# A one-element copy on GpSimd that waits for a key transfer, taken out ahead of the weight loads

## The chip, the core and the metric

The kernel runs on one core of a Trainium2 chip. The metric is the device time of one execution in microseconds; lower is better. A core has five engines that run their own instruction queues side by side: TensorE (PE, with its weight loads listed apart as PEld), VectorE (DVE), ScalarE (ACT), GpSimd (POOL) and SyncE (SP). Transfers between device memory and the on-chip buffer are issued from a queue of an engine (here nearly all from GpSimd's) and carried by 16 DMA engines.

## What is computed

A block-sorted attention followed by a gated feed-forward block. Batch 4, 8 heads, 768 positions in 8 blocks of 96, head size 64; then 3,072 tokens, width 512, hidden width 1,536.

```python
P = sort_net                                   # 4 x 8 x 8 x 8
for _ in range(5):                             # Sinkhorn
    P = exp(P - max(P)); P = P / rowsum(P); P = P / colsum(P)
k_sorted = einsum('bhij,bhjcd->bhicd', P, k_b)  # blocks of keys are mixed
v_sorted = einsum('bhij,bhjcd->bhicd', P, v_b)  # blocks of values are mixed
attn = softmax(scale * q_b @ k_sorted^T)        # inside each block
x = (attn @ v_sorted) as [3072 tokens, 512]
out = (silu(x @ w_gate) * (x @ w_val)) @ w_out
```

## The kernel before

The feed-forward works on eight tiles of 384 tokens (`ffn(n)`, n = 0 to 7: two for each batch). For each of 12 columns m of 128 hidden units it runs a gate product (`gate`, line 387), a value product (`value`, line 405), each four matmuls, with tanh on ACT (line 395) and two products on DVE (lines 397 and 410). The output products of tile n-1 (`outp`, line 422) are strewn between the columns of tile n, and so are the attention steps of the tiles that come next.

Ahead of the first tile stands an opening of some 22 us: the Sinkhorn steps on ACT and DVE, meanwhile the values of batch 0 land and are turned into a column-major copy `vch` by ACT (lines 203 to 220) and by GpSimd (lines 150 to 152). TensorE then mixes the values (`v_chunk`, line 277) and the keys (`k0_chunk`, line 266), and goes on to scores, softmax and the first columns of the feed-forward (`early`, line 521).

The order of the instructions of TensorE and GpSimd is the order in which they are written. Up to line 539 that of DVE and ACT is too; from line 540 on `manual_schedule` names TensorE and GpSimd alone, and DVE and ACT are ordered by the planner.

GpSimd's queue is the one to follow here. In order: two loads of batch 0's values (lines 144 and 145), the identity matrix, the first part of the queries (`load_q0(0)`), two loads of the keys of batch 0 (`k0`, lines 148 and 149, 384 KB each), three value copies (lines 150 to 152), a copy of one element per partition out of `k0` into a tile `landed` (line 154) that nothing reads, and then the transfers that follow: `load_gv` brings 256 columns of the gate weights and of the value weights (256 KB each, line 111), six such pairs in all, between them the second part of the queries (line 156), the values of batch 1 (line 159), and behind them keys and queries of batch 1 and the output weights (lines 162 to 164). A column pair m, m+1 of the feed-forward needs the pair of loads m/2: m = 8 and 9 need the fifth pair, m = 10 and 11 the sixth.

A transfer is issued in the queue's order. Each uses one of eight completion semaphores in turn, so in the profile a later issue can be seen to wait for a transfer eight places ahead: the issue at 24.12 us waits for the second part of the queries, issued at 16.35.

GpSimd comes back to copying values when those of batch 1 have landed (lines 597 and 598), and then issues the loads for batches 2 and 3.

Of the kernel before, what the change touches and what calls it, by code (L numbers as in the profile page):

```python
# [10 lines left out]
BF16 = mybir.dt.bfloat16  # L11
# [6 lines left out]
def kernel(  # L18
# [11 lines left out]
    nc = tc.nc  # L30

    B, H, S, D = q.shape
# [21 lines left out]
    const = ctx.enter_context(tc.tile_pool(name="const", bufs=1))  # L54
# [58 lines left out]
    def load_gv(lo, hi):  # L113
        load_w(wg_sb, wg_dram, lo, hi)
        load_w(wv_sb, wv_dram, lo, hi)

    def copy_v(eng, pair, rows, s, n=4, d0=0, d1=D):
        cs = slice(s * (C // n), (s + 1) * (C // n))
        dst = vch3[rows, d0:d1, cs]
        src = v_tiles[pair][rows, cs, d0:d1]  # L120
        if eng is nc.scalar:
            eng.copy(dst, src.transpose([0, 2, 1]))  # L122
        else:
            eng.tensor_copy(dst, src.transpose([0, 2, 1]))  # L124
# [8 lines left out]
    HC = C // 2  # L133
# [3 lines left out]
    k0 = qk0[:, 0:HC, :]  # L137
# [12 lines left out]
    copy_v(nc.gpsimd, 0, lowr, 0)  # L150
    copy_v(nc.gpsimd, 0, lowr, 3)
    copy_v(nc.gpsimd, 0, lowr, 5, 8, 40, D)
    landed = const.tile([128, 1], BF16)
    nc.gpsimd.tensor_copy(landed, k0[:, HC - 1, D - 1:D])
    load_gv(0, 256)
    load_q0(1)
    for m in range(256, 1024, 256):
# [499 lines left out]
```

## Time and profile before

| | us |
|---|---|
| median of 3 runs | 249.78 |
| lowest and highest of them | 249.61 and 251.17 |
| profiled execution, its own time | 251.09 |
| its span, first to last instruction | 249.0 |
| TensorE busy | 237.3 |
| VectorE busy | 157.7 |
| ScalarE busy | 110.7 |
| GpSimd busy | 52.1 |

The profile shows one execution. The span is counted from the first instruction to the last; the execution's own time is 2.1 us longer. Views that are used below: the page's busy times and its row of 40 slices (each digit a busy share in tenths), the chain of waits (followed back from the last instruction to what released each step), the timeline of one engine (start, length, and in brackets the idle time ahead with what ended it), and a table of busy times by stretch. Line numbers are those of the kernel.

The granted TensorE clock is 1.00 over the whole span.

### The profile page before, as it was taken

How to read it: one execution, taken by the hardware profiler on the slowest of the kernel's cores; microseconds unless marked ns; L12 is line 12 of the kernel's file. 1: busy time of each engine (PE TensorE's matmuls, PEld its weight loads, DVE VectorE, ACT ScalarE, POOL GpSimd, SP SyncE). 2: the span in 40 equal slices, each digit the busy share in tenths (PEclk: the TensorE clock that was granted, in tenths of full speed). 3: DMA queues.
4: the chain of work that ended last, by engine and by line, in shares of the span. 5: the costliest groups of instructions: out<-in, count | busy, mean ns of one | idle time of the engine just before them, and what ended most of it. 6: DMA issues, size and time to landing. Idle time of an engine off the chain costs nothing.

```text
span 249.0 us, 6163 instructions
## 1 busy us (share of the span) xinstructions
PE 237.3 (95%) x2609; PEld 140.8 (57%) x2633; DVE 157.7 (63%) x332; ACT 110.7 (44%) x186; POOL 52.1 (21%) x46
## 2 busy tenths in 40 slices
PE   6799998999999999999999999999999999999995
PEld 5375655676555556654555655555555555555543
DVE  6786888787556765857558547745764585446700
ACT  3977752353643444545742552353344343232411
POOL 5966439990039400000000000000000000000000
PEclk9999999999999999999999999999999999999999
DMA  5959999999999389110112121112111121100122
GB/s 98 211 72 181 212 192 219 198 223 217 213 175 187 64 184 156 35 42 3 45 32 74 45 74 34 43 42 73 37 42 45 32 61 58 42 14 32 42 80 89
DMA packets 39578, 24.38 MB, mean 98 GB/s; under 512 B 27712, under 2 KB 35648, under 8 KB 39104
## 3 DMA queue, kind: packets, MB, share of 16 engines
q0 software_dynamic: 21376, 14.16, 38.9%
q1 hardware_dynamic: 18176, 9.84, 14.6%
q8 instruction: 20, 0.33, 0.5%
q14 instruction: 6, 0.05, 0.0%
HBM read 28.32 MB, written 7.86 MB: 145 GB/s over the span
## 4 chain that ended last, share of the span: by engine, by line
PE 72%; DMA 14%; DVE 6%; issue 3%; POOL 3%; ACT 2%; DVEq 0%; POOLq 0%
PE o_ps L422 22%; PE v_ps L405 21%; PE g_ps L387 20%; DMA wv_sb<-in_moe_w_val_dram 6%; DMA qk<-in_k_dram 4%; DMA wg_sb<-in_moe_w_gate_dram 4%; PE tkq L246 3%; PE av_ps L336 2%; DVE gs_sb L397 2%; PE qk L309 2%; DVE h L410 1%; PE o_ps L438 1%; DVE st L342 1%; ACT th_sb L395 1%; DVE vt L224 1%
## 5 line engine op out<-in xcount | busy, mean ns | idle before, releaser
L397 DVE SCALAR_TENSOR_TENSOR gs_sb<-th_sb,g_ps 128x384 bf16<-128x384 bf16 x96 | 52.9, 551 | 51.8 <-ACT th_sb L395 48.9
L405 PE MATMUL v_ps<-xt,wv_sb 128*128 128x384 bf16 x380 | 77.3, 326 | 1.4 <-DMA wv_sb<-in_moe_w_val_dram 0.8
L387 PE MATMUL g_ps<-xt,wg_sb 128*128 128x384 bf16 x376 | 76.7, 326 | 1.1 <-DMA wg_sb<-in_moe_w_gate_dram 1.0
L395 ACT ACTIVATE th_sb<-g_ps 128x384 bf16<-128x384 f32 x96 | 47.1, 491 | 57.8 <-PE g_ps L387 53.9
L422 PE MATMUL o_ps<-wo_sb,h 128*128 128x512 bf16 x255 | 61.4, 379 | 1.3 <-issue 0.3
L410 DVE SCALAR_TENSOR_TENSOR h<-v_ps,gs_sb 128x384 bf16<-128x384 f32 x96 | 53.4, 556 | 7.0 <-PE v_ps L405 0.3
L405 PEld LDWEIGHTS <-wv_sb 128*128 128x128 bf16 x380 | 35.1, 97 | 25.3 <-issue 2.0
L387 PEld LDWEIGHTS <-wg_sb 128*128 128x128 bf16 x376 | 34.7, 97 | 24.6 <-DMA wg_sb<-in_moe_w_gate_dram 1.4
L422 PEld LDWEIGHTS <-h 128*128 128x128 bf16 x276 | 26.3, 98 | 28.9
L427 ACT COPY o_sb<-o_ps 128x512 f32<-128x512 f32 x23 | 13.5, 586 | 50.8 <-PE o_ps L422 50.8
L124 POOL COPY vch<-v 64x1536 bf16<-64x1536 bf16 (+2 forms) x11 | 28.6, 2648 | 20.8 <-PE o_ps L422 17.2
L322 ACT ACTIVATE e_all<-qk 96x768 bf16<-96x768 f32 x30 | 22.6, 802 | 7.7 <-PE qk L309 7.7
L342 DVE TENSOR_TENSOR st<-av_ps,r_sb 96x512 bf16<-96x512 f32 x32 | 21.7, 679 | 0.2
L336 PEld LDWEIGHTS <-e_all 96*128 96x128 bf16 x256 | 12.2, 98 | 4.9 <-ACT e_all L322 0.8
L336 PE MATMUL av_ps<-vt,e_all 96*128 96x65 bf16 x256 | 13.5, 194 | 0.1
L340 DVE RECIPROCAL r_sb<-av_ps 96x8 f32<-96x8 f32 x32 | 6.4, 199 | 8.8 <-PE av_ps L336 8.7
L224 DVE CAST vt<-tv 96x1024 bf16<-96x1024 f32 (+1 forms) x9 | 9.8, 1100 | 2.6 <-PE tv L287 1.6
L226 ACT CAST vt<-tv 96x1024 bf16<-96x1024 f32 (+1 forms) x9 | 9.2, 1031 | 2.9 <-PE tv L287 1.8
L448 PE MATMUL idle_ps<-warm_sb 128*128 128x512 bf16 x22 | 6.1, 381 | 0.3 <-issue 0.2
L224 DVE COPY oh_sb<-o_ps 128x256 f32<-128x256 f32 x1 | 0.4, 425 | 9.3 <-PE o_ps L438 9.3
L372 POOL DMA_DIRECT2D q_scr<-in_q_dram x2 | 5.7, 3225 | 0.0
L122 ACT COPY vch<-v 64x768 bf16<-64x768 bf16 (+1 forms) x4 | 5.4, 1389 | 0.2 <-DMA v<-in_v_dram 0.2
(81 smaller groups left out, 135.0 us busy)
## 6 DMA issues: line engine op xcount, KB each, us to landing
out_dram<-o_sb SPq DMA_DIRECT2D x23, 256.0 KB, 2.0
v<-in_v_dram POOLq DMA_DIRECT2D x3, 768.0 KB, 19.6
wg_sb<-in_moe_w_gate_dram POOLq DMA_DIRECT2D x6, 256.0 KB, 10.5
wv_sb<-in_moe_w_val_dram POOLq DMA_DIRECT2D x6, 256.0 KB, 11.4
wo_sb<-in_moe_w_out_dram POOLq DMA_DIRECT2D x1, 1536.0 KB, 24.0
kp<-in_k_dram POOLq DMA_DIRECT2D x2, 768.0 KB, 14.8
q_scr<-in_q_dram POOLq DMA_DIRECT2D x2, 768.0 KB, 29.7
v<-in_v_dram POOLq DMA_DIRECT2D x2, 384.0 KB, 5.5
```

The costliest lines, as they stand in the source:

```text
L124: eng.tensor_copy(dst, src.transpose([0, 2, 1]))
L224: nc.vector.tensor_copy(dst, src)
L322: nc.scalar.activation(e_all[:, n:n + 2, 0:4 * C], wide[0:C, :, 0:4 * C], AF.Exp, scale=scale)
L336: nc.tensor.matmul(o[:, two, i4, :], lhsT=e[:, i4 * C:i4 * C + 128], rhs=vt[:, 2 * g + two, half * 4 + i4, :], start=True, stop=True)
L342: nc.vector.tensor_tensor(st.rearrange("p i two d -> p two i d"), o[0:C, :, :, 0:D], r_sb.to_broadcast([C, 2, 4, D]), op=ALU.mult)
L387: nc.tensor.matmul(g_ps, lhsT=wg_sb[:, kc, ts(m, 128)], rhs=xt[:, kc, :], start=(kc == 0), stop=(kc == NKC - 1))
L395: nc.scalar.activation(th_sb, g_ps, AF.Tanh, scale=0.5)
L397: nc.vector.scalar_tensor_tensor(gs_sb, th_sb, 1.0, g_ps, op0=ALU.add, op1=ALU.mult)
L405: nc.tensor.matmul(v_ps, lhsT=wv_sb[:, kc, ts(m, 128)], rhs=xt[:, kc, :], start=(kc == 0), stop=(kc == NKC - 1))
L410: nc.vector.scalar_tensor_tensor(h_tiles[n][:, m, :], v_ps, 0.5, gs_tiles.pop(m), op0=ALU.mult, op1=ALU.mult)
L422: nc.tensor.matmul(o_ps, lhsT=h_w[:, m, ts(t3, 128)], rhs=wo_sb[:, m, :], start=(m == 0), stop=(m == NFC - 1))
L427: nc.scalar.copy(o_sb, o_ps)
```

## The change

The copy and the tile that it writes are taken out. The next instruction of GpSimd's queue behind the last value copy is then the first weight load.

```diff
     copy_v(nc.gpsimd, 0, lowr, 0)
     copy_v(nc.gpsimd, 0, lowr, 3)
     copy_v(nc.gpsimd, 0, lowr, 5, 8, 40, D)
-    landed = const.tile([128, 1], BF16)
-    nc.gpsimd.tensor_copy(landed, k0[:, HC - 1, D - 1:D])
     load_gv(0, 256)
     load_q0(1)
     for m in range(256, 1024, 256):
```

## The prediction

> **What bounds the kernel now.** I read the page first, then the chain of waits over the first 60 us, then GpSimd's and TensorE's timelines, and a table of stretches for the DMA. The page:
>
> ```profile
> PE 237.3 (95%) x2609; PEld 140.8 (57%) x2633; DVE 157.7 (63%) x332; ACT 110.7 (44%) x186; POOL 52.1 (21%) x46
> ...
> DMA  5959999999999389110112121112111121100122
> ...
> PE 72%; DMA 14%; DVE 6%; issue 3%; POOL 3%; ACT 2%; DVEq 0%; POOLq 0%
> ```
>
> TensorE is busy for 95% of the span, so whatever is won must come out of its 11.7 us of idle time. The DMA engines are full in the first third and nearly idle after it, and yet they own 14% of the chain. The chain shows where:
>
> ```profile
> 4.06 10.16 DMA qk<-in_k_dram
> ...
> 14.35 0.19 POOL landed L154
> 14.54 0.28 issue
> 14.82 0.80 POOL wg_sb L111
> ...
> 18.38 9.46 DMA wg_sb<-in_moe_w_gate_dram
> 27.84 0.28 issue
> 28.12 14.88 DMA wv_sb<-in_moe_w_val_dram
> 43.00 0.04 issue
> 43.04 0.82 PE v_ps L405 x4
> ```
>
> It runs from the load of the keys through the copy to be removed, through the weight issues, and ends in a value product at 43.04 that waits for its weights. So the copy stands on the path that sets the end. GpSimd's own timeline:
>
> ```profile
> 6.25 6.24 POOL L124 COPY vch<-v 64x1536 bf16<-64x1536 bf16 x3 [1.64 <-DMA v<-in_v_dram]
> 14.35 0.19 POOL L154 COPY landed<-qk 128x1 bf16<-128x1 bf16 x1 [1.87 <-DMA qk<-in_k_dram]
> 14.82 0.80 POOL L111 DMA_DIRECT2D wg_sb<-in_moe_w_gate_dram  x1 [0.28 <-issue]
> ```
>
> The copies end at 12.49, the next transfer is issued at 14.82: 2.33 us in which nothing is issued. What the DMA engines do meanwhile (the last two columns are their mean busy share and GB/s):
>
> ```profile
> 12.50:13.00 0.50, 0.50 (x24) 0.47 (x17) 0.02 (x1) 0.35 (x1) 0.00 (x0) 1.00 0.61 123
> 14.00:14.50 0.50, 0.50 (x23) 0.50 (x20) 0.50 (x1) 0.23 (x1) 0.15 (x1) 1.00 0.00 0
> 16.00:16.50 0.50, 0.50 (x44) 0.50 (x38) 0.50 (x1) 0.28 (x2) 0.50 (x2) 1.00 0.12 14
> 17.00:17.50 0.50, 0.41 (x16) 0.41 (x17) 0.50 (x2) 0.50 (x2) 0.50 (x1) 1.00 1.43 193
> ```
>
> The keys' bulk is over at 13.0, and the engines then move next to nothing until about 16.5, some 1.6 us behind the issue at 14.82. Last, what TensorE loses to it:
>
> ```profile
> 14.95 1.97 PE L266 MATMUL tk<-rmix,qk 128*64 128x64 bf16 x96
> ...
> 37.74 0.82 PE L387 MATMUL g_ps<-xt,wg_sb 128*128 128x384 bf16 x4 [0.99 <-DMA wg_sb<-in_moe_w_gate_dram]
> ...
> 39.05 0.82 PE L405 MATMUL v_ps<-xt,wv_sb 128*128 128x384 bf16 x4
> ...
> 43.04 0.82 PE L405 MATMUL v_ps<-xt,wv_sb 128*128 128x384 bf16 x4 [0.78 <-DMA wv_sb<-in_moe_w_val_dram]
> ```
>
> These are columns 8 and 10 of the first tile. The value product of column 8 starts 0.06 us behind the transpose before it (38.66 + 0.33 = 38.99), with its weight load held by the DMA. These are TensorE's only waits for a transfer in the whole span.
>
> **What the change does to the start of the stream.** Removed: a copy of 0.19 us and its wait of 1.87, with the 0.28 behind it. What stands between a value copy and an issue isn't shown at this place. Bounds: at 47.79 an issue follows a value copy with no gap, and at 14.54 the gap is 0.28. I take 0.28, the same pair of kinds (a copy, then this very issue). So the first weight issue goes from 14.82 to 12.77 (12.49 at best): 2.05 us earlier, at most 2.33. All issues up to line 164 move with it. Those that wait for a completion eight places ahead (24.12 for the second part of the queries, 25.45, 26.78 and 28.12 for the second pair of weights and the third gate load, 33.67 for the fourth value load) wait for transfers of the same stream, which moves as well. The third value load and the fourth gate load, issued at 19.11 and 19.84, reuse the keys' two semaphores and now need a wait of their own for the keys; at 17.06 and 17.79 these have long landed (14.22), so I cost it at nothing; without that cover it would be the old 2 us on part of the stream.
>
> **Whether the stream moves as a whole.** From 17 us on the share is above 0.9 in nearly every stretch, at 180 to 220 GB/s, up to about 60 us; a full queue that starts 2.05 us earlier ends 2.05 us earlier. One thing limits this: fetches of instructions (33 GB/s in 13.5 to 14.0, 16 in 15.5 to 16.0) fall into the empty stretch now, and would share with weights then. 33 GB/s x 0.5 us and 16 x 0.5 are 25 KB, 0.12 us at 200 GB/s if spread, but up to 0.5 us if they fall on one engine, since a transfer has landed only when its last engine has. So landings move by 1.5 to 2.3 us; I take 1.9, near the row of the issue.
>
> **What TensorE wins.** Column 8's gate: weights land at about 37.7, TensorE is free at 36.75 (35.94 + 0.81); a shift of 0.99 clears it. Column 8's value: 0.06. Column 10's value: landed at 43.00, TensorE free at 42.27 (41.93 + 0.34), and by then 1.05 earlier, so at 41.22; the weights land at 41.1 with a shift of 1.9 and at 41.5 with 1.5. So 0.77 is won, or 0.5 with the smaller shift. Sum: 0.99 + 0.06 + 0.77 = 1.82 us at best, 1.5 at the low end.
>
> DVE and ACT must keep up when the gaps close. In the 10 us before (26 to 36) TensorE was busy 10.00, DVE 9.10 and ACT 5.82 with the same sort of work; in 36 to 46 they were busy 8.05, 7.38 and 2.85. DVE's 7.4 us fit into 8.2, a load of 0.9 as before; I take off 0.1 for it. That leaves 1.7.
>
> **What comes late next.** Everything TensorE meets behind this is fed by the same stream. Values of batch 1 land at 36.6 (issued 21.55, 15.0 to land), GpSimd's four copies of them run from 36.72 to 47.85, and `v_chunk` starts at 48.75: a cover of 0.90, kept when both move by 1.7 to 2. Keys and queries of batch 1 land at 46.4 and 49.7 and are used at 53.96; the output weights land at 57.7 and are used at 59.29: covers of 4 and 1.6. If one of these didn't move while TensorE did, the output weights would cost 0.1 and the values 0.8. Behind 60 us GpSimd's loads for batches 2 and 3 move with its copies, and TensorE waits for no transfer.
>
> **The keys.** They land at 14.22 and `k0_chunk` loads its first operand at 14.74, right behind the value chunks: a cover of 0.52 us. With the change the first weight bytes come about 1.6 us behind 12.77, at 14.4, past the keys' landing. I cost the keys at nothing; their bound is the rival below.
>
> **A rule against it.** The row: the issue at 15.60 runs beside a DVE cast that starts at 15.69 and takes 0.76 us, and the issue at 25.45 takes 0.74; casts out of PSUM did not slow an issue. The Trainium skill, SBUF — State Buffer, section "SBUF: two separate sides", warns that a DVE operation in a two-port mode locks GpSimd out, so that descriptors aren't written and transfers start late. The earlier issues fall beside the value casts at 12.98 to 15.50, which the old ones escaped; if the rule applied to those, the first issue would be held to 15.5 and the gain would be nothing or below. The row decides for me: no hold.
>
> **The sum.** 249.0 - 1.7 = 247.3 of span, 251.09 - 1.7 = 249.4 of this execution's own time. That execution lay 1.3 above the median; against the median of 249.78 the forecast is 248.1, 0.7% less.
>
> **The rivals.**
> (a) Half of it: the stream's last engine gains only 1 us (fetches, or DVE late in releasing PSUM). Column 10's wait stays: 0.9 won, 248.9. For it: columns 8 and 10 wait for the last of 16 engines, which no view shows. Against: share above 0.9 throughout.
> (b) Nothing, because the issues are held by DVE's casts, or the DMA engines' stretch stays empty for another reason: 249.8. Against: the 0.76 row.
> (c) The keys late. If all of the first pair of weights (512 KB, 2.6 us at 200 GB/s) went ahead of the keys' last bytes, they would land at 16.8 and TensorE would lose 2.6 - 0.5 = 2.1 in the opening, where nothing covers it, and win 1.8 later: 250.1. From a delay of 2.3 us on the change would be a loss. Against it: weights are issued 8 us after the keys, and the keys are nearly through at 13.0.
> (d) Slower: from line 540 on DVE and ACT are ordered by the planner, and an instruction fewer ahead can turn that order. One DVE product (0.56 us, lines 397 and 410) put ahead of what TensorE waits for, in each of the eight tiles, costs 4.5, less 1.7: 252.6. It is a loss from 0.21 us a tile on. For it: DVE is at 0.9 in the first tile. Against: behind 26 us the view of waits has 0.8 us of TensorE's matmuls waiting for DVE, and none for ACT.
>
> **How the numbers follow.** Forecast 0.64, (a) 0.14, (b) 0.06, (c) 0.05, (d) 0.06; 0.05 for a win above 2.5 us, by an order that fell better. A measurement of this kernel can tell about 1% (2.5 us) from no change. Within 1% lie the forecast, (a), (b) and (c): 0.89, of which I give 0.02 to slower for a mixture with (d): faster 0.05, same 0.87, slower 0.08. Range: from 1.82 + 0.28 won (the shift at its bound), less another 0.3 for the spread of medians, 247.4, up to (c) at 250.1.
>
> **What would show it.** GpSimd issues the first weights at 12.5 to 12.8; the DMA share is up by 15; the keys land at 14.2 and line 266 starts at 14.95 as before; the three waits at 37.74, 39.05 and 43.04 are gone; from 46 us on everything is about 1.7 earlier, and the chain has no DMA between 18 and 43. I am wrong if line 266 starts later, if a DMA wait stays in columns 8 to 10, or if TensorE has new waits for DVE or ACT in the first tile.

## The result, and the profile after

| | before | after |
|---|---|---|
| median of 20 runs each, us | 251.07 | 248.88 |
| lowest and highest | 249.27 and 252.96 | 248.72 and 252.26 |
| ratio, 95% interval | | 0.9942 (0.9917 to 0.9966) |
| profiled execution, own time | 251.09 | 248.75 |
| its span | 249.0 | 246.8 |

The change makes the kernel faster by 0.6%, and less scattered: 17 of the 20 runs after lie between 248.7 and 249.4; those before are spread over 3.7 us. The medians differ by more than the ratio says (2.19 us, 0.9%), since the median of a kernel that scatters so much moves itself: in the later sets of runs the kernel before has medians from 250.2 to 251.0. Line numbers behind the removed lines are lower by two.

The page of the changed kernel (busy times, the DMA row of 40 slices, the chain by engine):

```profile
PE 238.7 (97%) x2633; PEld 140.8 (57%) x2633; DVE 157.2 (64%) x332; ACT 110.7 (45%) x186; POOL 52.0 (21%) x45
...
DMA  5999999999999395010121111112111211100122
...
PE 84%; DVE 7%; ACT 3%; issue 3%; DMA 2%; DVEq 0%; ACTq 0%; POOLq 0%
```

The third slice of the DMA row (12.3 to 18.5 us) has gone from 5 to 9, and the DMA's share of the chain from 14% to 2%. GpSimd's timeline of the changed kernel:

```profile
6.23 6.24 POOL L124 COPY vch<-v 64x1536 bf16<-64x1536 bf16 x3 [1.62 <-DMA v<-in_v_dram]
12.42 0.80 POOL L111 DMA_DIRECT2D wg_sb<-in_moe_w_gate_dram  x1
```

The first weights are issued at 12.42, right at the copies' end and 2.40 us earlier than before. TensorE's timeline of the changed kernel, at the places that the prediction named:

```profile
14.92 1.97 PE L264 MATMUL tk<-rmix,qk 128*64 128x64 bf16 x96
...
35.91 0.81 PE L403 MATMUL v_ps<-xt,wv_sb 128*128 128x384 bf16 x4
36.56 0.81 PE L385 MATMUL g_ps<-xt,wg_sb 128*128 128x384 bf16 x4
...
37.63 0.81 PE L403 MATMUL v_ps<-xt,wv_sb 128*128 128x384 bf16 x4
...
40.83 0.81 PE L403 MATMUL v_ps<-xt,wv_sb 128*128 128x384 bf16 x4
```

The key chunks start as before (14.95 then, 14.92 now). The gate product of column 8 is 1.18 us earlier, column 8's value product 1.42, column 10's 2.21, and the span is shorter by 2.2: the whole difference is made by 41 us, and all behind it moves as one piece. The instructions of TensorE, DVE, ACT and SyncE stand in the same order in both kernels; GpSimd's list is shorter by the copy.

### The profile page after: what moved, and what is told of

Its sections match the earlier page's. It is cut to its first block, busy times and chain, and to the rows that moved or that the text cites. A ratio compares the mean times of both kernels' runs of the same rounds, so it can differ in the third digit from the quotient of the medians.

```text
span 246.8 us, 6185 instructions
## 1 busy us (share of the span) xinstructions
PE 238.7 (97%) x2633; PEld 140.8 (57%) x2633; DVE 157.2 (64%) x332; ACT 110.7 (45%) x186; POOL 52.0 (21%) x45
## 4 chain that ended last, share of the span: by engine, by line
PE 84%; DVE 7%; ACT 3%; issue 3%; DMA 2%; DVEq 0%; ACTq 0%; POOLq 0%
PE v_ps L403 23%; PE o_ps L420 23%; PE g_ps L385 22%; PE av_ps L334 3%; PE tkq L244 3%; PE qk L307 3%; DVE gs_sb L395 2%; DMA v<-in_v_dram 2%; DVE h L408 1%; PE idle_ps L446 1%; PE tv L275 1%; PE o_ps L436 1%; DVE st L340 1%; PE x_ps L351 1%; ACT th_sb L393 1%
## 5 line engine op out<-in xcount | busy, mean ns | idle before, releaser
L420 PE MATMUL o_ps<-wo_sb,h 128*128 128x512 bf16 x276 | 64.0, 379 | 0.0
L425 ACT COPY o_sb<-o_ps 128x512 f32<-128x512 f32 x23 | 13.5, 586 | 50.8 <-PE o_ps L420 50.8
L334 PE MATMUL av_ps<-vt,e_all 96*128 96x65 bf16 x256 | 13.5, 194 | 0.0
L446 PE MATMUL idle_ps<-warm_sb 128*128 128x512 bf16 x25 | 6.9, 382 | 0.0
```

The source lines that it names most:

```text
L334: nc.tensor.matmul(o[:, two, i4, :], lhsT=e[:, i4 * C:i4 * C + 128], rhs=vt[:, 2 * g + two, half * 4 + i4, :], start=True, stop=True)
L420: nc.tensor.matmul(o_ps, lhsT=h_w[:, m, ts(t3, 128)], rhs=wo_sb[:, m, :], start=(m == 0), stop=(m == NFC - 1))
L425: nc.scalar.copy(o_sb, o_ps)
```

## The experiments

**The copy or the clock.** My theory: what counts is when the weight stream starts. The rival: the wait for the keys itself costs. Three kernels put other work in the copy's place, which waits for nothing; a fourth keeps the wait and moves one pair of loads ahead of it.

```diff
     copy_v(nc.gpsimd, 0, lowr, 5, 8, 40, D)
+    scr = const.tile([128, D, C // 4], BF16)
+    nc.gpsimd.tensor_copy(scr[lowr, 0:54], v_tiles[0][lowr, 0:C // 4, 0:54].transpose([0, 2, 1]))
     load_gv(0, 256)
```

With 54 columns this is `delay_2400ns`, with 24 `delay_1200ns`, with the 54-column line twice `delay_4800ns`.

> The changed kernel, with a value copy into an unused buffer on GpSimd (about 2.4 us by the rows of the other copies) in the place of the copy that waited for the keys; no wait. Theory (what counts is the moment at which the weight stream starts): first weight issue near 14.8 us, waits of TensorE for weights back in columns 8 and 10 of the first tile, span 248.4 to 249.6, time as the kernel before (ratio 0.997 to 1.003). Rival (it is the wait for the keys, or the semaphore it sets, that costs): span 246.8, ratio 0.994 or below.

> The same with a copy of about 1.2 us. Theory with a cover: in the changed kernel the last weights land 1.7 us ahead of their use, so a delay of 1.2 is hidden and the span stays at 246.8 to 247.2. Rival 1 (linear: each us of delay is a us of time): span 247.9. Rival 2 (the lag of the stream's last DMA engine differs from run to run by up to 2 us, as between the two profiles): span up to 248.1, and times that scatter more than those of the changed kernel.

> The changed kernel with about 4.8 us of copies into an unused buffer ahead of the first weight issue. Theory (start of the stream, past its cover a us for a us): first issue near 17.2, 2.4 us later than in the kernel before, span 251.0 to 251.8, ratio to the kernel before 1.007 to 1.011. Rival (behind column 10 other things bound, so the loss levels off): span below 250.5.

Measured: 2.4 us of delay give a ratio of 1.0026 (0.9985 to 1.0066) to the kernel before, the same time, with no wait for any key. TensorE's timeline of that run has the waits for weights back, in the same two places:

```profile
37.11 0.82 PE L387 MATMUL g_ps<-xt,wg_sb 128*128 128x384 bf16 x4 [0.27 <-DMA wg_sb<-in_moe_w_gate_dram]
...
42.04 0.82 PE L405 MATMUL v_ps<-xt,wv_sb 128*128 128x384 bf16 x4 [0.36 <-DMA wv_sb<-in_moe_w_val_dram]
```

Its span, 248.0, fell below what I had written (248.4 to 249.6). With 1.2 us of delay the span is 247.0, hidden as the cover said, but eleven of the twelve times run from 248.74 to 251.55, the scatter that my second rival had named; the ratio, 0.9966 (0.9931 to 1.0001), can be told neither from the kernel before nor from the change. In this profile the cover was just enough; that it fell short in the longer runs is likely, but they have no profile. With 4.8 us the ratio is 1.0084 (1.0045 to 1.0122), in the expected band, but the span of 250.1 lies where the rival had put it (below 250.5, the loss levels off). There the first issue is 3.08 us later than before and the last weights land only 0.6 later; TensorE's 2.5 us of waits for weights all lie ahead of column 10, which finds its weights landed. So a us of delay was not a us of time. The rival of the wait falls by the run with 2.4 us: no wait, a start near the old one, the old time.

```diff
+    load_gv(0, 256)
     landed = const.tile([128, 1], BF16)
     nc.gpsimd.tensor_copy(landed, k0[:, HC - 1, D - 1:D])
-    load_gv(0, 256)
     load_q0(1)
```

> The kernel before, but with the first pair of weight loads (512 KB) issued ahead of the copy that waits for the keys; the wait itself stays. Theory (the stream's start counts): 512 KB feed the DMA engines for 2.6 us from 14 us on, the copy ends at about 14.5 and the next issue comes before they run dry; span 246.8 to 247.4, ratio as the changed kernel. Rival (the wait on the keys costs, wherever it stands): span near 249.0.

Measured: 0.9938 (0.9910 to 0.9966), span 246.8. The copy may stay, as long as something is queued ahead of it. It hardly waits any more, though: GpSimd is busy with the two issues up to 14.41 and runs the copy at 14.49, so the run shows that the copy and its place ahead of the rest of the stream cost nothing, not what a long wait would cost.

**One profile of before was not the kernel before.** Both kernels were profiled a second time, unchanged.

> The kernel before, unchanged: a second profile of it. Theory (its time hangs on the last of the DMA engines to land the weights): waits for weights in columns 8 and 10 of another length than 0.99 and 0.78, all times of this run scattered by 2 us and more. Rival (the scatter is from elsewhere): the same waits, and a span that differs all the same.

> The changed kernel, unchanged: a second profile and interval. Theory: no wait of TensorE for weights, span 246.8 to 247.2, scatter below 1 us in most runs, ratio 0.990 to 0.996.

Measured: the kernel before had a span of 247.3 this time, and no wait of TensorE for weights long enough for its list; its ratio to itself was 1.0004 (0.9968 to 1.0040), its 12 runs from 249.26 to 252.68. The changed kernel had 247.2 and 0.9950 (0.9923 to 0.9978). GpSimd's issues and the times to landing, with TensorE's timeline, give one table for all of this (the last weights are the sixth value load; landed is its issue plus its time to landing, when the last of the 16 DMA engines is through):

| run | first weights issued | last weights landed | column 10's value starts | span | span less that start |
|---|---|---|---|---|---|
| before | 14.82 | 43.0 | 43.04 | 249.0 | 206.0 |
| before_again | 15.06 | 41.3 | 41.30 | 247.3 | 206.0 |
| delay_4800ns | 17.90 | 43.6 | 43.99 | 250.1 | 206.1 |
| delay_2400ns | 15.17 | 42.0 | 42.04 | 248.0 | 206.0 |
| delay_1200ns | 14.19 | 41.1 | 41.09 | 247.0 | 205.9 |
| after | 12.42 | 39.1 | 40.83 | 246.8 | 206.0 |
| after_again | 12.89 | 40.9 | 40.93 | 247.2 | 206.3 |

The last column says that the kernel is rigid behind 41 us; the span is that one start plus 206. The third says that the landing is no fixed distance behind the first issue: 28.2 us in one profile of before and 26.2 in the other, 26.7 and 28.0 in the two after. In the landing records of that load the 16 engines' parts end from 38.98 to 43.00 us in the first profile of before, twelve of them by 40.26, and from 36.70 to 39.10 in the change: the last engine is what TensorE waits for. TensorE needs the weights at 40.8 at the earliest, so before is exposed to all of this scatter and after to its tail. That the times of the other runs scatter for this reason fits, but is not shown: they have no profile.

**Pushing it further, and a new stop.** If the first issue may come earlier, GpSimd has 1.6 us to spare while it waits for the values.

```diff
+    load_gv(0, 256)
     copy_v(nc.gpsimd, 0, lowr, 0)
     copy_v(nc.gpsimd, 0, lowr, 3)
     copy_v(nc.gpsimd, 0, lowr, 5, 8, 40, D)
-    load_gv(0, 256)
     load_q0(1)
```

> The changed kernel with the first pair of weight loads issued ahead of the value copies, in the 1.6 us in which GpSimd waits for the values of batch 0 (4.6 to 6.2 us); the transfers still queue behind the keys. Theory: the copies start at 6.2 to 6.3 as before, the stream goes on from 13.1 with no gap, the last weights land about 1.2 us earlier than in the changed kernel; its TensorE had no wait for weights left, so the span is 246.6 to 247.0 and only the scatter of times may shrink. Rival (weights queued this early hold up the keys or the copies): line of the key chunk starts later than 14.95, span above 247.5.

Measured: span 247.9, ratio 0.9974 (0.9947 to 1.0000), 1.1 us worse than the change alone, though its 12 runs lie within 0.54 us (249.72 to 250.26). The last weights land at 37.7, the key chunks start at 14.95 as ever. Neither theory had this (TensorE's timeline of `pair_early`):

```profile
14.95 1.88 PE L264 MATMUL tk<-rmix,qk 128*64 128x64 bf16 x91
18.01 0.26 PE L264 MATMUL tk<-rmix,qk 128*64 128x64 bf16 x5 [1.18 <-issue]
```

TensorE stops for 1.18 us behind 91 of 96 matmuls that all have what they need; "issue" says that the trace shows nothing that it waits for. The DMA answer by stretch has a candidate. First the changed kernel from 13 to 14 us, then `pair_early` from 15 to 16 (packets, MB, and the share of the 16 engines' time in that stretch, as the view adds it up):

```profile
q0 software_dynamic: 6, 0.01, 6.6%
q8 instruction: 1, 0.02, 5.5%
```

```profile
q0 software_dynamic: 271, 0.21, 134.2%
q8 instruction: 1, 0.02, 5.9%
```

One packet of 16 KB of instructions runs at 13.6 us in the changed kernel, when the other queue is nearly silent. With 512 KB of weights queued ahead, no such packet shows from 13 to 15; it comes at 15.6. The Trainium skill, Runtime: NRT & Kernel Launch, section "Instruction fetch mechanics", says that a sequencer refills its instructions by a DMA queue of its own in blocks of 16 KiB, 256 instructions, and that crossing a border is mostly hidden. If this stop is such a border, here it was not hidden. A matmul with its weight load is two instructions, so borders would lie 128 matmuls apart. That can be tested without touching any transfer: change the number of matmuls ahead, and the stop must move by as many. Both tries stand on `pair_early`; `dots` are small warm-up matmuls, `fill` large ones.

```diff
     dots(124)
-    for it, n in ((1, 3), (2, 4), (3, 4), (4, 4)):
+    for it, n, more in ((1, 1, 17), (2, 1, 26), (3, 1, 26), (4, 2, 17)):
...
         fill(idle_ps, n)
+        dots(more)
```

> The kernel with the first weight pair issued ahead of the value copies (pair_early: TensorE stopped for 1.2 us before the 92nd matmul of the key chunks, with nothing that it waited for), with TensorE's warm-up changed: 10 of 15 large throwaway matmuls replaced by 86 small ones of the same total length, so every later instruction stands 76 matmuls further back in TensorE's queue. Theory (the stop is a fetch of TensorE's next 16 KB of instructions, which queues behind the weights on its DMA engine): the stop leaves the place 91 of 96, since the border between two fetches moves to another matmul; key chunks in one piece from 14.95, span 246.6 to 247.0, times within 0.6 of each other. Rival (the stop belongs to the key chunks: PSUM, keys or an operand): it stays at the 92nd matmul, span 247.9.

Measured: the stop left the key chunks. But the small matmuls did not hold the clock (granted 0.74 from 8 to 10 us, 0.50 from 10 to 18), so the time, 1.0092 (1.0063 to 1.0120), says nothing of the stop, and the expected span was missed by 3.7 us. A stop of 0.62 us, which I had not forecast, stood behind the first matmul of the first av step (TensorE's timeline of `early_shifted`):

```profile
22.00 0.20 PE L334 MATMUL av_ps<-vt,e_all 96*128 96x65 bf16 x1
22.83 0.40 PE L334 MATMUL av_ps<-vt,e_all 96*128 96x65 bf16 x7 [0.62 <-issue]
```

Counted from the first key matmul that is 96 + 16 + 4 + 24 + 2 + 1 = 143; worked out afterwards, the border belongs at 91 + 128 - 76 = 143. The second try takes matmuls away and keeps the clock:

```diff
-    dots(124)
+    dots(48)
+    fill(idle_ps, 9)
```

> The kernel with the first weight pair ahead of the value copies again, with 76 of the 124 small warm-up matmuls replaced by 9 large ones of the same total length (the run with 86 small ones more had lost half of TensorE's clock): 67 matmuls fewer ahead of all else, the clock kept at 1.00. Theory (a border every 128 matmuls, at each of which 16 KB of instructions must have come): the border behind 91 matmuls of the key chunks moves to 158, the sixth matmul of the second av step, the one before it to 30; a stop, if there is one, stands behind the 30th matmul of the key chunks or the 158th counted from their first, and nowhere else before 23 us. Rival (the stop belongs to the key chunks' last matmuls): behind the 91st again.

Measured, TensorE's timeline of `early_shifted2`:

```profile
14.95 0.66 PE L264 MATMUL tk<-rmix,qk 128*64 128x64 bf16 x30
17.81 1.23 PE L264 MATMUL tk<-rmix,qk 128*64 128x64 bf16 x66 [2.20 <-issue]
```

The stop stands behind the 30th matmul, where the border was computed before the run, and it is longer. The clock was 1.00 up to the stop and fell behind it (granted 0.50 from 20 to 22), so this stop cost more than its length: 1.0135 (1.0104 to 1.0166), and there was another stop of 0.9 us later at line 244, 639 matmuls behind the first, one short of five times 128. So the stop stands at a border in TensorE's instructions. That it lasts until the next 16 KB have come fits the packets: TensorE goes on 2.3 to 2.4 us behind the start of one in all three runs (15.6 and 18.01 in `pair_early`, 20.4 and 22.83 in `early_shifted`, 15.5 and 17.81 in `early_shifted2`). In the changed kernel 13.6 and 2.4 make 16.0, ahead of the 91st key matmul's end at some 16.8, and there is no stop.

Why the packet comes late is not shown. My theory was that it waits for all the weights queued ahead on its DMA engine, and 13.6 without them against 15.5 and 15.6 with them fits. But in `early_shifted`, with the same two loads queued ahead, a packet ran at 13.5 to 13.6 in the midst of weights (its DMA answer from 13 to 14 us):

```profile
q0 software_dynamic: 352, 0.19, 136.2%
q8 instruction: 1, 0.02, 5.6%
```

The trace names neither the DMA engine of a packet nor whose instructions it holds.

**Half of it.** One load is queued ahead instead of two.

```diff
+    load_w(wg_sb, wg_dram, 0, 256)
     copy_v(nc.gpsimd, 0, lowr, 0)
...
-    load_gv(0, 256)
+    load_w(wv_sb, wv_dram, 0, 256)
     load_q0(1)
```

> Only the first gate load (256 KB) goes ahead of the value copies, its value load stays behind them. Theory (the fetch of instructions waits for what is queued ahead of it): 256 KB keep the DMA engines busy to about 14.4 instead of 15.7, but the issue at 12.5 keeps them busy behind it too, so the fetch that ran at 13.6 in the changed kernel starts between 14.4 and 15.6 and TensorE stops for 0 to 1.2 us at the same matmul; span 246.8 to 247.9. Rival (no fetch involved; what counts is two issues ahead of the copies): span 247.9 or 246.8 with no stop and a fetch at 13.6.

> The kernel with the first gate load alone ahead of the value copies, a second time. Theory (its last weights land 3 to 4 us ahead of their use, twice the cover of the changed kernel, and the fetch of instructions still comes in time): span 246.8 to 247.0, all times within 0.5 of each other, ratio 0.990 to 0.996.

Measured: spans 246.9 and 246.8, no stop. The instruction packet runs in 13 to 14 us, not between 14.4 and 15.6 as I had written, and here too in the midst of weights (`half_early` from 13 to 14 us):

```profile
q0 software_dynamic: 354, 0.18, 133.4%
q8 instruction: 1, 0.02, 5.6%
```

No stop and an early packet were the rival's sign. What the rival says of the stop, that no fetch is involved, does not fit its moving with the count of matmuls; but the theory of the packet's delay missed here. The last weights land at 37.4 and 37.2, 3.6 us ahead of their use at 40.96 and 40.83. The first set of 11 runs lies between 248.72 and 248.90, ratio 0.9931 (0.9904 to 0.9959); the second has median 248.80, ten of 11 between 248.73 and 249.14, ratio 0.9911 (0.9880 to 0.9942). By the intervals it can't be told from the change itself in the mean. Its 22 runs have one above 249.2, the change's 32 have nine: it scatters less, though not as little as I had written for the second set (249.76 is 1.0 above the lowest), and the two kernels were not run in the same set.

**The keys late.** The last one builds my rival (c): weights ahead of the keys.

```diff
     load_q0(0)
+    load_gv(0, 256)
     for a, rows in enumerate(halves):
         nc.gpsimd.dma_start(out=k0[rows], in_=k_nat[0, :, a * HC:(a + 1) * HC, :])
```

(The same pair is taken out behind the copies.)

> The changed kernel with the first pair of weight loads issued ahead of the loads of the keys: the case that the copy would guard against, in full. Theory (nothing covers the opening beyond 0.5 us): keys land at about 16.7 instead of 14.1, the key chunk starts 1.8 to 2.1 us later than at 14.92, span 248.6 to 249.0. Rival (the opening has more slack than the profile shows): span below 247.5.

Measured: 1.0063 (1.0038 to 1.0089) to the kernel before, median 252.10, 3.1 us above the changed kernel's 249.03 of the same set. The profiled run, the longest of its 13 (span 252.4), shows the keys landing at 17.1 and the key chunks starting at 17.23, 2.3 us late, close to what I wrote. The span is 3.4 us above the 249.0 that I had put as the most, and the clock is a part of why (stretches of two us of `pair_before_keys`; the granted clock is the third number from the right):

```profile
14.00:16.00 2.00, 0.84 (x29) 0.71 (x25) 1.52 (x2) 1.61 (x3) 2.00 (x4) 0.96 1.01 208
16.00:18.00 2.00, 0.77 (x29) 0.80 (x31) 0.00 (x0) 0.26 (x1) 2.00 (x4) 0.50 1.12 193
...
20.00:22.00 2.00, 2.00 (x21) 0.73 (x15) 1.66 (x5) 0.69 (x2) 1.15 (x2) 0.50 1.45 196
```

TensorE idles 2.39 us for the keys and then runs at half its clock up to 22 us; the first transposes of the attention stand at 25.57 instead of 21.50, so 2.3 us of keys became 4.1 us. Column 10's value starts at 46.47, 5.6 us late, and the span is that plus 205.9, the same rigid rest. Nearly all of the other 1.6 us stand in two lines of this run's timelines, DVE's and TensorE's:

```profile
31.03 2.44 DVE L536 COPY rmix<-ident 64x64 bf16<-64x64 bf16 x1
...
34.58 0.51 PE L307 MATMUL qk<-kqt 64*128 64x96 bf16 x16 [1.49 <-DVE kqt L222]
```

The same small copy takes 0.17 us in the changed kernel, at 26.96, well ahead of GpSimd's copies of batch 1's values (from 34.00). Here these start at 30.57, ahead of it, and TensorE waits 1.49 us for the DVE cast that comes after it. That GpSimd's copy holds up DVE's is read from the times alone; no run tests it. The median of this kernel is 2.3 us below this run, so the whole account is that of one execution.

## Why the prediction was right, and where it was wrong

- **The mechanism** held at each point that I had named: the issue at 12.4, the DMA's stretch filled from 15 us on, the keys' chunk unmoved, the three waits gone, no DMA in the chain between 18 and 43 us, everything behind it earlier by one amount. The first issue came a little ahead of the 12.5 to 12.8 that I had named, and the shift was 2.2 us, not 1.7. The run with 2.4 us of other work shows that it is the stream's start and nothing else of the copy.
- **What failed: the step "A measurement of this kernel can tell about 1% (2.5 us) from no change."** I put 0.87 on a time within 1%, and it came there, but I treated such a gain as one that can't be seen. Twenty runs of each kernel give an interval of a quarter of a per cent to either side, and it leaves out 1: the kernel is faster. The second set says the same (0.9950, 0.9923 to 0.9978). By my own sum (0.7%) I should have called it so.
- **The sum of 1.7 us was mis-sized in two places that pull apart.** In this pair of profiles it is 2.2. I read TensorE's idle time off as start less the last group's start and length (36.75, 38.99 and 42.27 for its being free). The lengths overlap the next group by 0.16 us: in the changed kernel the gate of column 8 starts 0.65 behind the value product's start (35.91 to 36.56), whose group is 0.81 long. Three waits, three times 0.16, are 0.5, which gives 2.3; less the 0.1 for DVE that I had taken off it is the 2.2 that was found. (The 11.7 us of idle time, from which I started, were too many as well: the page of before has 2609 matmuls beside 2633 weight loads, so some matmuls were not recorded. The sum does not use it.)
- **But the waits themselves were one draw.** My terms came from a profile of before whose last weights landed at 43.0. In the second one they landed at 41.3, and against that the changed kernel wins 0.5 us. Over many runs the gain is 0.58%, about 1.45 us of 250, between the two; the forecast ratio (248.1 over 249.78, 0.993) lies inside the interval. That it does is in part luck: my one profile had a late landing, and the overlap that I missed pulled the other way. The table of three runs, 249.61 to 251.17, held the warning: a spread of 1.6 us in a kernel whose rest is rigid.
- **The stream's shift.** I took 2.05 for the issue, from a gap of 0.28 behind a copy; the gap was none and the shift 2.40, a little above my bound of 2.33. The landing moved by 3.9 in this pair, not 1.9, for the reason just given. My estimate of what instruction fetches would do (0.12 to 0.5 us to the weights) was too small for one engine: the packet at 13.6 takes 7.3% of the 16 engines' time in a us of the profile of before, 1.2 us of one engine. And it looked at one side only: what a fetch costs the weights no run shows, but in `pair_early` a packet came 2.0 us later and TensorE stopped. In the change it ran just ahead of the weights, at 13.6.
- **The rule against it** did not bite: the issues at 12.42 and 13.20, beside DVE's value casts, took 0.80 and 0.76 us, the same as the first two of before. I had misread one of these: the old issue at 14.82 had not escaped the value casts, which run from 12.98 to 15.50, so a row of 0.80 us beside them was there already.
- **The rivals.** (a) and (b) did not come in the profile. (c), priced at 2.1 us for the opening, costs 4.1 in its profiled run, in which the clock falls. (d) falls outright: the order of DVE and ACT is the same.

## What to carry to other kernels

A queue that is kept from issuing costs nothing until the last transfer of the stream is late; then TensorE loses what the landing is late by, which here was less than the delay (an issue 5.5 us later than in the changed kernel, with `delay_4800ns`, cost 3.3 us of span). So follow the stream to its last user and compare landing and use in more than one profile. Give such a stream cover beyond its usual lag: the best times hardly move (248.72 in the change and in `half_early`), and fewer runs are long. When loads are queued earlier, look at the instructions' packets too: 16 KB of them last for 128 matmuls with their weight loads, under 3 us at the pace of the key matmuls (96 in 1.97 us).

## What was not expected of the hardware

- With 512 KB of weights queued ahead, a packet of 16 KB of instructions ran 2.0 us later (15.6 for 13.6), and TensorE stopped for 1.18 us, or 2.20 where the border lay 61 matmuls earlier. The stop is entered as "issue", at a place fixed by the count of instructions: behind 91 matmuls from the first key matmul, then 143 (worked out afterwards) and 30 (forecast). What makes a packet late is open: others ran at 13.5 to 13.6 and at 13.9 in the midst of weights.
- After a stop of 1.18 us the granted clock stayed at 1.00; after 2.20 and 2.39 us it fell to 0.50 for some us. It fell as well in a warm-up with more small and fewer large matmuls. No run tried a length between 1.18 and 2.20.
- The last of the 16 engines lands the sixth value load 26.2 to 28.2 us behind the first issue of the weights, in runs of the same two kernels. What makes one engine lag was not found.
- A copy of 64x64 on DVE took 2.44 us for 0.17 elsewhere, in the one profile in which GpSimd's large copies had started ahead of it.
